# Gated attention with a mixture of experts: the lists of tokens added up by matrix products, routing in two batches, and a new order of the attention's steps

## Chip, cores and metric

One core of one Trainium2 chip runs the whole program. The metric is the time of one execution in microseconds of the device (us), as the median of several runs. Lower is better.

## What is computed

A recurrent attention (4 batches, 8 heads, 768 steps, head size 48) writes 3072 rows of 384 numbers, and each row then goes through the one of 8 experts that its gate picks:

```python
for t in range(S):
    S_re, S_im = ar*S_re - ai*S_im + outer(k[t], v[t]), ar*S_im + ai*S_re
    y[t] = q[t] @ S_re                 # rows x of the second half
e_idx = argmax(x @ w_gate, 1)
for e in range(8):
    m = e_idx == e
    out[m] = gate_w[m] * eom[m, e] * (relu(x[m] @ w1[e]) @ w2[e])   # 384 -> 1024 -> 384
```

gate_w is the softmax weight of the chosen expert and eom a sigmoid gate. The inputs are float32; products of the experts are made of a high and a low part of each factor.

## The kernel before

The rows are cut into 24 chunks of 128 (chunk 0 to 23, six to a batch). For each chunk the attention takes some fifty steps, each a Python function of one to 48 instructions: loads (la, lb), the logarithms of the decay (Ln, Ex, D1, Sq, L1, D2, E2, D3), running sums on TensorE (cd, cp), sines and cosines, the products of k and q with them (kc, qc), their transposes (trk, trq) and the copies of these out of PSUM (ck, cq), scores (sc), the mask (mk), the state (st, sd, cps), the output (va), its copy (xt), the product that gives rows and gate logits (ro), and then the copy of the rows (xn), their store to DRAM (xs) and the sum of the logits (gt). A table written out by hand (ORDER) lists the steps; every engine takes its instructions in this order. A letter v or a behind a step moves a copy to VectorE, or a rounding or an absolute value to ScalarE.

Routing stands in the same table. Chunks 0 to 19 are routed in BATCHES of 6, 6, 6 and 2. For each batch, R1 to R4 (choose and weigh) find on VectorE each row's expert, its rank among that expert's rows, and its gate weight; two matrix products (R2) count the rows before it. GpSimd then works out the row's address in a table in DRAM (pl: places), and writes one pair (row id, gate weight) per row with an indirect DMA, one per chunk (el: enter_list). K1 to KV rank the experts by size. Before the first expert starts, rr reads its list back (read_ranked), si makes ids of it, and ga fetches the rows with four indirect DMAs. Chunks 20 to 23 (the TAIL) are added in another way: P1, PK, P2 make 0/1 rows, fl adds their rows to the first expert's input by matrix products, and lists/add put their entries in the other lists after the first expert has begun. After the attention, TensorE runs the experts one after another (experts: up_products, down_products), and the other lists are read from DRAM.

Six PSUM banks are handed round between the steps in the order of the table, so a step that holds a bank for long keeps the next from starting. Two constants used below: NS = 4 slots to a list row, NP = 116 list rows.

Of the kernel before, what the change touches and what calls it, by code (L numbers as in the profile page):

```python
# [1535 lines left out]
```

## Time and profile before

| | us |
|---|---|
| median of 3 runs | 484.17 |
| lowest and highest run | 483.86, 489.08 |
| the profiled execution | 489.85 |
| its span, first to last instruction | 488.1 |

The profiled execution is 1.75 us longer than its span, and 5.68 us longer than the median. Busy shares of the span: PE (TensorE matrix products) 95%, PEld (its weight loads) 86%, DVE (VectorE) 70%, ACT (ScalarE) 62%, POOL (GpSimd) 25%. A busy PE is a modelled figure, since matrix products overlap; the share of PEld tells better how full TensorE is. The granted clock was at the higher of its two levels (2.4 GHz) throughout, but for the last slice. The attention fills the time up to about 246 us, the experts the rest.

### The profile page before, as it was taken

The page shows a single profiled execution, that of the slowest core. Times are in us where ns is not written, and L with a number is a line of the kernel's source. Part 1 is how long each engine was busy: PE and PEld are TensorE (multiplying, and loading weights), DVE is VectorE, ACT ScalarE, POOL GpSimd, SP SyncE. Part 2 cuts the span into 40 slices and gives each one's busy share as a digit, 9 for nine tenths or more (in the row PEclk, how much of TensorE's full clock was granted, in tenths as well). Part 3 has the DMA queues.
Part 4 walks back from the last instruction along what each step waited for, and adds up shares of the span by engine and source line. Part 5 has one row for each costly group of instructions (what it writes and reads, how often), then busy time and mean ns, then how long its engine had stood idle before and what let it go on. Part 6 is the DMA issues. An engine that isn't in the chain of part 4 may idle for free.

```text
span 488.1 us, 11400 instructions
## 1 busy us (share of the span) xinstructions
PE 466.0 (95%) x4350; PEld 418.9 (86%) x4350; DVE 340.6 (70%) x693; ACT 304.4 (62%) x569; POOL 123.0 (25%) x161
## 2 busy tenths in 40 slices
PE   8998999899999979999999999999999999999991
PEld 4786777778888768888888999999999999999991
DVE  4499999999999979998799764362735536283210
ACT  7759889989998768743266565362735536283330
POOL 5100000013300540183401645324251222021112
PEclk9999999999999999999999999999999999999997
DMA  8974354524543231003835789283552817220001
GB/s 277 319 234 133 97 153 127 178 81 108 95 162 99 67 67 36 34 19 132 266 111 185 187 240 296 69 252 110 151 181 59 279 49 243 69 92 26 25 25 49
DMA packets 47757, 65.66 MB, mean 135 GB/s; under 512 B 11711, under 2 KB 39498, under 8 KB 47668
## 3 DMA queue, kind: packets, MB, share of 16 engines
q1 hardware_dynamic: 39540, 55.01, 36.9%
q0 software_dynamic: 8128, 9.42, 6.9%
q8 instruction: 62, 1.02, 0.9%
q14 instruction: 27, 0.22, 0.1%
HBM read 53.92 MB, written 9.88 MB: 131 GB/s over the span
## 4 chain that ended last, share of the span: by engine, by line
PE 57%; DVE 17%; issue 16%; POOL 4%; ACT 2%; DMA 1%; POOLq 0%; another core or an unknown queue 0%; SPq 0%; DVEq 0%; ACTq 0%
PE b L1208 8%; PE b L186 7%; PE b L1193 6%; PE xo L1193 6%; PE b L668 5%; PE st L1208 4%; POOL out_dram L1227 3%; DVE scores L673 3%; PE xo L700 3%; PE b L338 2%; PE b L613 2%; PE xo L706 2%; PE st L683 2%; PE st L861 2%; DVE kc L645 2%
## 5 line engine op out<-in xcount | busy, mean ns | idle before, releaser
L1227 POOL DMA_INDIRECT out_dram<-y,sid x28 | 33.3, 1190 | 116.9 <-ACT y L1249 113.4
L668 PE MATMUL b<-qt,kt 96*128 96x128 f32 x384 | 48.3, 279 | 1.7 <-ACT qt L657 1.3
L668 PEld LDWEIGHTS b<-qt,kt 96*128 96x128 f32 x384 | 44.9, 192 | 5.3 <-ACT qt L657 2.0
L1097 POOL DMA_INDIRECT rows<-xd,sid x28 | 35.1, 1255 | 51.4 <-DVE gate L1080 24.9
L1290 DVE SCALAR_TENSOR_TENSOR hl<-xo,hh 128x464 fp32r<-128x464 f32 (+7 forms) x32 | 18.9, 589 | 38.4 <-ACT hh L1289 29.2
L1290 DVE SCALAR_TENSOR_TENSOR hl<-b,hh 128x464 fp32r<-128x464 f32 (+7 forms) x32 | 18.9, 590 | 37.9 <-ACT hh L1289 33.3
L1289 ACT ACTIVATE hh<-b 128x464 fp32r<-128x464 f32 (+7 forms) x32 | 16.5, 517 | 37.5 <-PE b L1193 34.9
L1208 PE MATMUL b<-hh,w2h 128*128 128x392 f32 (+6 forms) x112 | 38.5, 344 | 0.0
L1208 PE MATMUL b<-hh,w2l 128*128 128x392 f32 (+6 forms) x112 | 38.4, 343 | 0.0
L1289 ACT ACTIVATE hh<-xo 128x464 fp32r<-128x464 f32 (+7 forms) x32 | 16.6, 520 | 33.4 <-PE xo L1193 26.3
L700 PE MATMUL xo<-scores,v 128*48 128x128 f32 x384 | 36.2, 277 | 1.0 <-DVE scores L673 1.0
L585 POOL COPY rcs<-rcs 24x48 f32<-24x48 f32 (+2 forms) x10 | 3.7, 373 | 126.3 <-DMA rcs<-re 81.6
L1193 PE MATMUL b<-xh,w1h 128*128 128x392 f32 (+6 forms) x93 | 33.6, 361 | 0.0
L1193 PE MATMUL xo<-xh,w1h 128*128 128x392 f32 (+6 forms) x93 | 32.9, 353 | 0.0
L673 DVE TENSOR_TENSOR scores<-b,mask 128x512 f32<-128x512 f32 x48 | 31.7, 680 | 1.4 <-PE b L668 0.7
L1193 PE MATMUL b<-xl,w1h 128*128 128x392 f32 (+6 forms) x93 | 31.6, 340 | 0.0
L1193 PE MATMUL xo<-xl,w1h 128*128 128x392 f32 (+6 forms) x93 | 31.6, 340 | 0.0
L1193 PE MATMUL xo<-xh,w1l 128*128 128x392 f32 (+6 forms) x93 | 31.6, 339 | 0.0
L1193 PE MATMUL b<-xh,w1l 128*128 128x392 f32 (+6 forms) x93 | 31.5, 339 | 0.0
L706 PE MATMUL xo<-qt,state 96*48 96x128 f32 x320 | 31.2, 272 | 0.2 <-DVE state L688 0.2
L318 DVE TENSOR_TENSOR w2l<-raw,w2h 128x512 fp32r<-128x512 f32 x42 | 26.6, 686 | 4.3 <-ACT w2h L317 4.3
L318 DVE TENSOR_TENSOR w1l<-raw,w1h 128x512 fp32r<-128x512 f32 x42 | 26.6, 686 | 4.2 <-ACT w1h L317 4.2
(281 smaller groups left out, 1320.3 us busy)
## 6 DMA issues: line engine op xcount, KB each, us to landing
raw<-in_moe_w_dram SPq DMA_DIRECT2D x32, 768.0 KB
ar<-in_a_re_dram SPq DMA_DIRECT2D x24, 192.0 KB
ai<-in_a_im_dram SPq DMA_DIRECT2D x24, 192.0 KB
q<-in_q_dram SPq DMA_DIRECT2D x24, 192.0 KB
k<-in_k_dram SPq DMA_DIRECT2D x24, 192.0 KB
v<-in_v_dram SPq DMA_DIRECT2D x24, 192.0 KB
xd<-xn SPq DMA_DIRECT2D x24, 192.0 KB
rows<-rows SPq DMA_DIRECT2D x1, 768.0 KB
```

The costliest lines, as they stand in the source:

```text
L186: return nc.tensor.transpose(out=out, in_=in_, identity=ident[p0:p0 + n, p0:p0 + n])
L318: nc.vector.tensor_tensor(out=lo[:, s], in0=raw[:, s], in1=hi[:, s].bitcast(F32), op=ALU.subtract)
L668: nc.tensor.matmul(sp[:, j * P:(j + 1) * P], cats_t["k"][i % 2][:D2, h, :], cats_t["q"][i % 2][:D2, h, :], start=True, stop=True)
L673: nc.vector.tensor_tensor(out=scores[i % 2][:, 4 * hh:4 * hh + 4, :], in0=of(("sc", i, hh)).rearrange("p (h t) -> p h t", t=P), in1=mask.u ...
L700: nc.tensor.matmul(op[u * DP:u * DP + D, j * P:(j + 1) * P], vt[:, h * D:(h + 1) * D], scores[i % 2][:, h, :], start=True, stop=(cc == 0))
L706: nc.tensor.matmul(op[u * DP:u * DP + D, j * P:(j + 1) * P], xs[:D2, h * D:(h + 1) * D], cats_t["q"][i % 2][:D2, h, :], start=False, stop= ...
L1097: ins = nc.gpsimd.indirect_dma_start(out=rows[e % 2][:n, i, :], out_offset=None, in_=xd[:known], in_offset=bass.IndirectOffsetOnAxis(ap=id ...
L1193: nc.tensor.matmul(used(up[:, :sizes[e]], n), w[:, kt, :], used(x[:, kt, :], n), start=(m == 0), stop=(m == 3 * KT - 1))
L1208: nc.tensor.matmul(used(accs[kt][:, :sizes[e]], n), w[:, cs], used(a, n), start=(ft == 0 and s == 0), stop=(ft == FT - 1 and s == 2))
L1227: ins = nc.gpsimd.indirect_dma_start(out=out, out_offset=bass.IndirectOffsetOnAxis(ap=id_of(e, i, n, loaded), axis=0), in_=y[:n, :], in_of ...
L1289: nc.scalar.activation(out=hh, in_=up[:, :cap], func=AF.Relu)
L1290: nc.vector.scalar_tensor_tensor(out=hl, in0=up[:, :cap], scalar=0.0, in1=hh.bitcast(F32), op0=ALU.max, op1=ALU.subtract)
```

## The change

The lists no longer go through DRAM. Each row has a list row `row` and a column `col` (expert and slot). GpSimd makes a 0/1 matrix of columns and multiplies it with three values (row id, high and low part of the gate weight); ScalarE makes a 0/1 matrix of list rows as relu(1 - |iota - row|) (step ir); TensorE adds up the product of the two over the chunks of a batch in one bank (Lp), and VectorE takes it over (Ld). Batches are now 18 and 2 chunks. si picks the first expert's list out of it, and in_places the others'; the last expert's list alone still takes a way through DRAM. ORDER is a new table; which copies go to which engine has changed in it as well: on VectorE 5 ck fewer, 7 cq more, 6 xn fewer, 2 cps more, 1 xt fewer, and 1 rounding and 4 absolute values more, with the opposite on ScalarE.

```diff
-BATCHES = ((0, 6), (6, 6), (12, 6), (18, 2))
+BATCHES = ((0, 18), (18, 2))
...
+set.0 la.0.0.0 la.1.0.0 la.0.0.1 la.2.0.0 la.1.0.1 la.2.1.1 Ln.0.0 la.2.1.0 Ln.1.0 la.2.0.1 Ex.0.0 lb.0.0 Ex.1.0 lg
...
+        if halves:
+            c = slice(c0, c0 + n)
+            nc.vector.tensor_copy(out=gate_hi[:, c], in_=entry[:, c, 1])
+            nc.vector.tensor_tensor(out=gate_lo[:, c], in0=entry[:, c, 1], in1=gate_hi[:, c].bitcast(F32), op=ALU.subtract)
...
             def pl(b):
-                places(sml, *BATCHES[b], eng=nc.gpsimd)
+
+                c0, n = BATCHES[b]
...
+                eng.tensor_tensor(
+                    out=at_, in0=iota[:, :E * NS].unsqueeze(1).broadcast_to([P, n, E * NS]),
+                    in1=col.unsqueeze(2).broadcast_to([P, n, E * NS]), op=ALU.subtract)
+                eng.tensor_scalar(out=at_, in0=at_.bitcast(F32), scalar1=0.0, scalar2=None, op0=ALU.is_equal)
...
+            def ir(b):
...
+                for i in range(n):
+                    function(out=is_row[:, i, :], in_=iota[:, :NP], func=AF.Abs, bias=row[:, i:i + 1])
+                function(out=is_row, in_=far, func=AF.Relu, scale=-1.0, bias=b_one)
...
             def el(b):
-                enter_list(*BATCHES[b])
...
+                for x, val in enumerate((entry[:, c, 0], gate_hi[:, c].bitcast(F32), gate_lo[:, c])):
+                    nc.gpsimd.tensor_tensor(
+                        out=cols[:, :, x, :], in0=is_col, in1=val.unsqueeze(2).broadcast_to([P, n, E * NS]), op=ALU.mult)
+
+            def Lp(b):
...
+                for c in range(n):
+                    nc.tensor.matmul(
+                        sp[:NP, :3 * E * NS], is_row[:, c, :], cols[:, c].rearrange("p x y -> p (x y)"),
+                        start=(c == 0), stop=(c == n - 1))
...
-            def rr():
-                read_ranked(0, 1)
-
             def si():
+                part = sml.tile([P, NS, E], F32, name="part")
+                nc.vector.tensor_tensor(
+                    out=part[:NP], in0=listed_by[:NP, 0].rearrange("p e i -> p i e"),
+                    in1=is_at[:NP, 0, :].unsqueeze(1).broadcast_to([NP, NS, E]), op=ALU.mult)
+                nc.vector.tensor_reduce(out=slots[:NP, 0, :, 0], in_=part[:NP], axis=AX.X, op=ALU.add)
                 slot_ids(0, 1)
...
-                for k in range(KT):
-                    turned(out=new_whole[:, k, :], in_=by_slot[:, k * P:(k + 1) * P])
...
-            for ins in read_ranked(1, E):
-                behind(ins, tail["gathered"])
...
+            def in_places(pool):
+
+                nc.vector.tensor_tensor(out=listed_by[:NP, 1], in0=listed_by[:NP, 1], in1=listed_by[:NP, 2], op=ALU.add)
+                part = pool.tile([P, E, NS, E], F32, name="part")
+                shape = [NP, E, NS, E]
+                for x in range(2):
+                    nc.vector.tensor_tensor(
+                        out=part[:NP], in0=listed_by[:NP, x].rearrange("p e i -> p i e").unsqueeze(1).broadcast_to(shape),
+                        in1=is_at[:NP].unsqueeze(2).broadcast_to(shape), op=ALU.mult)
+                    nc.vector.tensor_reduce(out=slots[:NP, :, :, x], in_=part[:NP], axis=AX.X, op=ALU.add)
```

GpSimd, before, from the routing of the third batch to the fetch of the first expert's rows:

```order
L1038 TENSOR_TENSOR row<-row,shift 128x6
L1039 TENSOR_SCALAR addr<-row 128x6
L1043 DMA table<-entry,addr 3712x2 x6
L793 MEMSET rows_2847 128x384
L1032 TENSOR_SCALAR row<-rank 128x2
...
L1043 DMA table<-entry,addr 3712x2 x2
L1097 DMA rows_2847<-xd,sid 116x384 x4
```

GpSimd, after, the same place: no table is written, and wide element-wise work stands there (cols is the matrix of columns, 18 chunks of 32).

```order
L781 TENSOR_TENSOR col<-col,off 128x18
L785 TENSOR_TENSOR cols_2628<-iota,col 128x18x32
L788 TENSOR_SCALAR cols_2628<-cols_2628 128x18x32
L808 TENSOR_TENSOR cols_2628<-cols_2628,entry 128x18x32
L808 TENSOR_TENSOR cols_2628<-cols_2628,gate_hi 128x18x32
L808 TENSOR_TENSOR cols_2628<-cols_2628,gate_lo 128x18x32
...
L1152 DMA rows_2951<-xd,sid 116x384 x4
```

The 20 table writes are gone, and five operations over 576 elements and five over 64 have come.

TensorE, after, around the adding up of the first 18 chunks (row 816; L687 is the state of chunk 21, L338 the rows of chunk 20, L672 scores):

```order
L183 MATMUL b_219<-ident,kc_198 96x128 x4
L687 MATMUL st<-v,kc_199 32x48 x24
...
L374 MATMUL b_215<-run,ones_b 128x16
L338 MATMUL b_217<-comb,xt_210 128x112 x4
L816 MATMUL b_219<-cols_2628,is_row_2715 116x96 x18
L672 MATMUL b_218<-qt_205,kt_203 128x128 x4
```

Whatever TensorE has to do for chunks 21 to 23 now stands behind these 18 products, which need GpSimd's cols and ScalarE's is_row.

TensorE, before, at the end of the attention (L668 scores, the last ones; L338 the rows of chunks 20, 21, 22, 23; L700 and L706 the output; L910 the transposes of the first expert's fetched rows):

```order
L668 MATMUL b_213<-qt_200,kt_198 128x128 x4
L338 MATMUL b_211<-comb,xt_206 128x112 x4
L338 MATMUL b_212<-comb,xt_207 128x112 x4
L700 MATMUL xo<-scores_204,v 48x128 x2
...
L338 MATMUL b_210<-comb,xt_206 128x112 x4
...
L338 MATMUL b_213<-comb,xt_207 128x112 x4
L910 MATMUL b_211<-ident,rows_2847 128x64 x8
```

TensorE, after, the same place:

```order
L338 MATMUL b_218<-comb,xt_211 128x112 x4
L672 MATMUL b_217<-qt_205,kt_203 128x128 x4
L672 MATMUL b_214<-qt_205,kt_203 128x128 x4
L704 MATMUL xo<-scores_208,v 48x128 x2
...
L338 MATMUL b_219<-comb,xt_210 128x112 x4
...
L338 MATMUL b_217<-comb,xt_211 128x112 x4
L967 MATMUL b_214<-ident,rows_2951 128x64 x4
```

The rows of chunks 20 and 21 now come ahead of the last scores, so that two of four such products are left between those and the transposes.

## Rows read from the trace of the kernel before

**Rows 1.** Busy time of each engine by stretch (stretch, its length, then the engines).

```profile
12.00:40.00 28.00, 27.80 (x365) 22.07 (x363) 20.98 (x37) 19.47 (x36) 1.90 (x5) 1.00 0.79 258
40.00:200.00 160.00, 152.72 (x1887) 125.61 (x1886) 152.12 (x288) 140.42 (x246) 24.23 (x34) 1.00 0.38 105
200.00:234.00 34.00, 32.67 (x491) 29.16 (x490) 31.83 (x83) 15.90 (x32) 16.42 (x24) 1.00 0.20 63
234.00:246.00 12.00, 10.64 (x161) 9.36 (x160) 8.71 (x35) 4.15 (x9) 5.31 (x4) 1.00 0.81 275
246.00:440.00 194.00, 193.70 (x1164) 189.86 (x1164) 112.26 (x225) 104.02 (x211) 61.37 (x50) 1.00 0.54 161
```

**Rows 2.** VectorE's waits over the span: for whom, us in total, times, longest.

```profile
DVE ai L624 <- ACT rnd L331: 4.6, 4, 3.3
```

**Rows 3.** VectorE in the four stretches that route the third batch of 6 chunks.

```profile
199.36:200.97 1.61, 1.40 (x9) 1.00 0.66 245
...
sum 2.91, DVE 2.57; mean DVE 0.64
```

**Rows 4.** VectorE's copies by form: count, busy us, mean ns.

```profile
L657 DVE COPY kt<-b 96x512 f32<-96x512 f32 x21 | 14.1, 678 | 0.0
L657 DVE COPY xn<-b 128x384 f32<-128x384 f32 x15 | 8.2, 544 | 0.0
L631 DVE TENSOR_SCALAR rnd<-ai 128x384 int32<-128x384 int32 x12 | 4.2, 346 | 0.0
```

**Rows 5.** GpSimd's groups: the table writes, and the wide operations that it has.

```profile
L1043 POOL DMA_INDIRECT table<-entry,addr x20 | 24.8, 1239 | 18.3 <-DVE scores L673 11.9 <-issue 4.9 <-DVE st L657 1.3
L231 POOL TENSOR_SCALAR_AFFINE_SELECT comb<-comb 128x192 f32<-128x192 f32 x2 | 1.2, 616 | 0.0
L215 POOL IOTA iota<- 128x464 f32 x1 | 0.5, 517 | 0.0
L199 POOL CAST tri_r<-tri_l 128x128 fp32r<-128x128 f32 x1 | 0.3, 279 | 0.0
```

**Rows 6.** All engines in order of time (start, us): two operations that meet.

```profile
199.58 0.21 DVE L354 TENSOR_TENSOR dl<-logits,mx 128x48 f32<-128x48 f32 x1
...
199.81 0.21 POOL L585 COPY rcs<-rcs 24x48 f32<-24x48 f32 x1 [21.70 <-PE b L186]
199.82 0.27 DVE L356 SCALAR_TENSOR_TENSOR ge<-dl,desc 128x48 f32<-128x48 f32 x1
```

**Rows 7.** GpSimd in order of time: first and last address operation of the third batch.

```profile
205.73 0.84 POOL L1032 TENSOR_SCALAR row<-rank 128x6 f32<-128x6 f32 x1 [5.70 <-DVE rank L378]
...
209.46 1.46 POOL L1039 TENSOR_SCALAR addr<-row 128x6 uint32<-128x6 f32 x1
```

**Rows 8.** ScalarE's groups by form.

```profile
L537 ACT ACTIVATE sq<-ai 128x384 f32<-128x384 f32 x5 | 2.6, 523 | 0.6 <-DVE ai L533 0.4
...
L331 ACT ACTIVATE ex<-dl 128x48 f32<-128x48 f32 x3 | 0.7, 241 | 0.0
```

**Rows 9.** TensorE in order of time, end of the attention and start of the experts.

```profile
234.92 1.94 PE L338 MATMUL b<-comb,xt 128*128 128x112 f32 x16
...
245.86 1.58 PE L910 MATMUL b<-ident,rows 64*128 64x64 f32 x20
...
248.60 0.28 PE L926 MATMUL b<-row,k 128*128 128x208 f32 x1
248.71 0.28 PE L926 MATMUL b<-row,q 128*128 128x208 f32 x1
...
276.84 0.92 PE L186 MATMUL b<-ident,rows 110*128 110x110 f32 x8
```

**Rows 10.** GpSimd in order of time: the first expert's fetches (first, last), the second's first.

```profile
235.31 1.37 POOL L1097 DMA_INDIRECT rows<-xd,sid  x1 [8.06 <-DVE sid L1076]
...
240.22 1.31 POOL L1097 DMA_INDIRECT rows<-xd,sid  x1 [0.30 <-issue]
266.41 1.07 POOL L1097 DMA_INDIRECT rows<-xd,sid  x1 [24.88 <-DVE gate L1080]
```

More of the change, by code (lines that the diff above doesn't have):

```diff
@@ L387, in at_once, with weigh @@
                 return end.value
[L389 removed]
+    def weigh(pool, c0, n, dl, oh, tag="", halves=False):
         def small(name, shape):
@@ L762, in pl @@
             def pl(b):
-                places(sml, *BATCHES[b], eng=nc.gpsimd)
-            def el(b):
-                enter_list(*BATCHES[b])
+                c0, n = BATCHES[b]
+                c = slice(c0, c0 + n)
+                pool = early if b < len(BATCHES) - 1 else sml
+                row, col, off = [pool.tile([P, n], F32, name=name) for name in ("row", "col", "off")]
+                eng = nc.gpsimd
+                eng.tensor_scalar(
+                    out=row, in0=rank[:, c], scalar1=-1.0 / NS, scalar2=0.5 - 0.5 / NS, op0=ALU.mult, op1=ALU.add)
@@ new lines, in pl @@
+                eng.tensor_scalar(out=row, in0=row, scalar1=ROUND, scalar2=-ROUND, op0=ALU.add, op1=ALU.add)
+                eng.tensor_scalar(out=off, in0=row, scalar1=float(NS), scalar2=float(E * NS), op0=ALU.mult, op1=ALU.add)
+                eng.tensor_scalar(out=col, in0=first[:, c], scalar1=float(-NS), scalar2=None, op0=ALU.mult)
+                eng.tensor_tensor(out=col, in0=col, in1=rank[:, c], op=ALU.add)
+                eng.tensor_tensor(out=col, in0=col, in1=off, op=ALU.add)
+                pool = early if b < len(BATCHES) - 1 else sml
@@ new lines, in pl @@
+                cols = pool.tile([P, n, 3, E * NS], F32R, name=f"cols{n}")
+                at_ = cols[:, :, 2, :]
+                eng.tensor_tensor(
+                    out=at_, in0=iota[:, :E * NS].unsqueeze(1).broadcast_to([P, n, E * NS]),
+                    in1=col.unsqueeze(2).broadcast_to([P, n, E * NS]), op=ALU.subtract)
+                eng.tensor_scalar(out=at_, in0=at_.bitcast(F32), scalar1=0.0, scalar2=None, op0=ALU.is_equal)
+                tail["list", b] = row, cols
+            def ir(b):
+                n = BATCHES[b][1]
+                row, _ = tail["list", b]
+                is_row = (early if b < len(BATCHES) - 1 else sml).tile([P, n, NP], F32R, name=f"is_row{n}")
+                far = is_row.bitcast(F32)
+                for i in range(n):
+                    function(out=is_row[:, i, :], in_=iota[:, :NP], func=AF.Abs, bias=row[:, i:i + 1])
+                function(out=is_row, in_=far, func=AF.Relu, scale=-1.0, bias=b_one)
+                tail["rows", b] = is_row
@@ L1012, in lists @@
                     pass
+                in_places(pool)
                 yield
@@ L1015, in lists @@
                 slot_ids()
+                ready["second rows"] = gather(1, CAPS[1])
+                slot_gates()
+                nc.sync.dma_start(
+                    out=by_rank.rearrange("(p s) y -> p s y", s=NS), in_=slots[:KT * P // NS, E - 1])
+                nc.sync.dma_start(out=whole, in_=by_rank.rearrange("(k p) y -> p k y", p=P))
+                yield
                 nc.vector.tensor_scalar(
                     out=whole_sid, in0=whole[:, :, 0], scalar1=float(NONE), scalar2=None, op0=ALU.add)
-                ready["second rows"] = gather(1, CAPS[1])
-                slot_gates()
                 yield
@@ L1308, in experts @@
                     if loaded and e == 0:
-                        for _ in range((0, 2, 1, 0, 0, 0, 0, 0)[ft]):
+                        for _ in range((0, 2, 1, 0, 0, 0, 1, 0)[ft]):
                             next(last)
```

199 lines of the change are left out of this document (98 added, 101 removed).

## The prediction

> **What bounds the kernel now.** I read the busy times by stretch first [rows 1], to see which engine has no time left where. From 246 to 440 us, in the experts, TensorE's weight loads are busy for 189.86 of 194 us: TensorE is full, and its work there is hardly touched. So the change can act only through the moment at which the experts start, and the reader is to look at the attention. There, from 40 to 200 us, VectorE is busy for 152.12 of 160, while weight loads fill 125.61 and ScalarE 140.42; from 200 to 234 VectorE has 31.83 of 34 and ScalarE only 15.90. VectorE bounds the attention, and a microsecond of its work is worth nearly one of the total. It stands still for 7.0 us between 12 and 40, 7.9 between 40 and 200, 2.2 between 200 and 234 and 3.3 between 234 and 246, 20.4 in all; a new order can win back only from these. Next I read its waits [rows 2]: the longest single one, 3.3 us at the start, is for a rounding on ScalarE. Last, the order of time at the end of the attention [rows 9, 10]: what stands between the last scores (234.9) and the transposes of the first expert's rows (245.86), a chain of small steps with VectorE a quarter idle.
>
> **The change part by part.** *Routing on VectorE.* One batch of 6 takes 15 small operations, which hold VectorE for 2.91 us, as four stretches show [rows 3]; three such batches take 8.7. One batch of 18 replaces them, again 15 operations, of which 11 read or write 144 elements a row for 48. The slope is that of the copies: (678 - 544) ns over 128 elements, 1.05 ns each [rows 4], so 0.10 us more for each of the 11: 2.9 + 1.1 = 4.0. New are four operations for the halves of the gate weights and four that take the lists over (Ld twice, si twice), small ones at the 0.2 that an operation of that stretch takes: 1.6. Together 5.6 for 8.7: -3.1 us. Bounds: -3.8 if the new ones hide in dependent waits, -2.0 if each takes 0.35.
>
> *Copies that change engines.* An operation holds VectorE for about 0.1 us less than its duration, since the next starts before it ends. Widths of 512: -5 ck, +7 cq, -1 xt, +1 at 0.58; of 384: -6 xn, +2 cps, +1 rounding, -3 at 0.44; +4 absolute values at 0.25 [rows 4]. 0.58 - 1.32 + 1.0 = +0.3 us. ScalarE gets the opposite, which its 18 idle us between 200 and 234 hide.
>
> *GpSimd's work, and what it does to VectorE.* Twenty table writes of 1.24 us go [rows 5]; nobody but the first list's read waited for them, so that alone is worth nothing. Ten element-wise operations come, five of them over 576 elements. The trace has none like these. From below, iota: 517 ns for 464 elements, 1.1 ns each, 0.64 us for 576; from above, the select: 616 ns for 192, 3.2 ns each, 1.85 us. I take the cast, 279 ns for 128, 2.2 ns each, 1.26 us, which like the new operations reads SBUF, without the select's pattern. Four of the five have two inputs. Where GpSimd and VectorE meet, the trace shows both slowed: a 48-wide step of VectorE took 0.27 beside a GpSimd copy, its neighbour of the same width 0.21 [rows 6]; GpSimd's address operations over 6 elements ran from 0.84 to 1.46 beside VectorE's products [rows 7]. With operations of 0.2 us this cost VectorE nothing; with 1.26 us it can. In the stretch of pl.0 and el.0, VectorE has five products of 768 with both inputs in SBUF (kc, qc) and some small ones. Nothing is lost if none of them meets a wide operation, and five times 1.26, 6.3 us, if each of the five wide ones holds VectorE for all its length. I take a quarter, +1.5, nearer to the row of 0.06 lost than to a full block.
>
> The Trainium skill has a rule that speaks against the change here: by "SBUF — State Buffer", section "Who interferes with whom", a VectorE instruction with two SBUF inputs and a GpSimd instruction that reads SBUF exclude each other for the whole of the one that started first. The trace agrees as far as its 0.06 us goes, and no run shows a wide operation. By that rule each of the five would hold VectorE for half its length on average, 3.2 us, and the whole sum below would be -0.9 in place of -2.6, 483.3 us.
>
> *ScalarE's matrix of list rows (ir.0).* 18 operations over 116 elements and one over 2088. With (523 - 241) ns over 336 elements, 0.84 ns each [rows 8], a short one lasts 0.30, and 0.2 where they overlap; the long one takes 1.95. In all 5.6 to 7.4 us, during which the copies ck.21.1, xt.20 and ck.22.1 queue behind it on ScalarE. The order leaves it about 6.5 (VectorE's work in that place, next paragraph, less what precedes ir.0). I take +0.3, between 0 and +1.5.
>
> *TensorE's 20 products (Lp).* 208-wide products of the same kind follow each other by 0.11 us [rows 9]: 2.2 us. They lie in a stretch in which weight loads leave 4.8 of 34 us free: 0, or +2.2 if that cover is gone. What matters is their wait. Behind the 18 on TensorE stand the scores and transposes of chunks 21 to 23, and for these all of VectorE's rest. They need GpSimd's five wide operations. From the rank of the 18 chunks to that place VectorE has five products of 768 (0.85 each), a 384-wide product, two sd, two cps and an xn (0.44), three copies and two masks (0.58) and some 15 small operations (0.2): 12.4 us. GpSimd needs six small operations, which go by the 5.2 us of the seven before [rows 7], 4.4, and five at 1.26 with 0.1 between: 11.2. So TensorE does not wait, with 1.2 us to spare.
>
> *End of the attention.* Two of the four products that make rows (16 instructions, 1.94 us [rows 9]) move from behind the last scores to before them, where TensorE has room. VectorE's share of this (the sums and low parts of chunks 20 and 21, about 1 us) moves as well, and there VectorE has none. 1.94 - 1.0: -1.0 us, between -2.5 and +0.5. What could be late next are the fetched rows: ids, then four fetches that last 6.2 us from 235.31 to 241.53 [rows 10]. Before, transposes followed 10.5 us after the first fetch; the shorter end leaves some 9.5, still more than fetches and landing need by TensorE's start. The list no longer goes through 8 table writes, a read of the table and the register with the expert's number; that takes waits off a path that had none on TensorE.
>
> *Start.* k is loaded ahead of q and the first rounding goes to VectorE itself; of the 3.3 us wait [rows 2] I count -0.3, between -2 and +0.5.
>
> *Experts.* Three transposes go, at 0.11: -0.3. in_places adds about 1.4 us to VectorE before the fetch for the second expert, now at 266.41 [rows 10]; its transposes stand at 276.84 [rows 9], and VectorE is busy for 112 of 194: nothing, or +1 if that fetch lands last.
>
> The sum: -3.1 + 0.3 + 1.5 + 0.3 - 1.0 - 0.3 - 0.3 = -2.6 us. It is made on the profiled execution, 489.85, giving 487.25. The median is 484.17; no row tells where the other 5.68 us went, so I carry the difference over: 481.6 us.
>
> **Rivals.** *GpSimd is late, and the attention waits at the 18 products.* If the wide operations cost the select's 1.85 us, with 0.1 between, they last 9.8; with 4.4 for the small ones 14.2; and if five of them first wait for a product of VectorE (0.95), 18.9. It decides from the 12.4 us at which TensorE arrives: then VectorE has nothing left that needs no scores, and 6.5 us are lost in place of the +1.5: -2.6 - 1.5 + 6.5 = +2.4, 486.6. For it speak the 1.46 us for 6 elements [rows 7]; against it, that GpSimd wins as many of these meetings as it loses, and that at the cast's price it is done in time.
>
> *The new order closes VectorE's gaps.* The 20.4 idle us [rows 1] come from waits like that of 3.3. If a fourth of them goes, 5.1 us, in place of the -1.3 taken for start and end, the sum is -6.4: 477.8. For it speaks that ScalarE has less to do late and that two batches fewer hand products between TensorE and VectorE; against it, that between 40 and 200 only 7.9 us are idle.
>
> *Nothing comes of it.* If VectorE's saved work only turns into longer waits for TensorE and ScalarE (busy for 140 of 160), 484.2.
>
> **How the numbers follow.** The forecast has 0.5, its own range -4.5 to +0.5 (479.7 to 484.7); closed gaps 0.24; nothing 0.13; GpSimd late 0.13. About 1%, 4.8 us, is what a measurement of this kernel tells from no change. Faster by more: all of the closed gaps but a fifth (0.19), and 0.08 of the forecast's tail: 0.27. Slower by more: the GpSimd case needs 7.4 us where it gives 2.4, some 0.06 of its 0.13, with 0.02 for an order that waits elsewhere: 0.08. Same: 0.65. The range takes in the closed gaps to -7.4 and the late GpSimd to +2.4: 476.8 to 486.6.
>
> **What would show it.** Right: VectorE's busy time before the experts about 3 us lower and its share still above 90% up to the last scores; the 18 products starting without a wait on GpSimd; the wide operations at 0.9 to 1.6 us; transposes of the first expert's rows 2 to 3 us earlier. Wrong: an idle VectorE of several us around 215 to 225 that ends with the 18 products; products kc and qc longer than 0.95 there; transposes that wait for a fetch; an expert stretch longer than before.

## The result, and the profile after

| | before, us | after, us |
|---|---|---|
| median of 20 runs each | 485.41 | 491.22 |
| lowest and highest | 482.75, 489.08 | 487.54, 496.22 |
| the profiled execution | 489.85 | 493.61 |
| first transposes of the experts' rows | 245.86 | 246.57 |

The ratio of after to before is 1.0107, 95% interval 1.0076 to 1.0138: about 1% slower, where 481.6 us and "within 1%" had been forecast. One thing is needed to understand it: the executions of the kernel before fall into two groups, 482.8 to 484.2 and 485.3 to 489.1 us here (an earlier and a later time below), sets of runs differ in which is the commoner, and the profile that the prediction read, 489.85, goes with the later; those of the kernel after spread without such a gap.

Busy time by stretch of the kernel after, columns as in [rows 1]:

```profile
12.00:40.00 28.00, 28.00 (x359) 22.44 (x357) 20.90 (x36) 20.63 (x40) 1.81 (x4) 1.00 0.85 288
40.00:200.00 160.00, 153.27 (x1874) 128.61 (x1873) 150.54 (x259) 139.57 (x241) 10.82 (x8) 0.98 0.34 104
200.00:234.00 34.00, 32.20 (x503) 28.96 (x502) 32.27 (x88) 20.94 (x50) 15.81 (x23) 1.00 0.17 61
234.00:246.00 12.00, 10.82 (x167) 9.97 (x167) 9.70 (x39) 6.64 (x15) 5.43 (x4) 1.00 0.88 286
246.00:440.00 194.00, 191.16 (x1135) 186.73 (x1135) 110.83 (x222) 98.78 (x201) 59.72 (x48) 0.99 0.54 159
```

Between 40 and 200 VectorE (third number with a count) is idle for 9.5 us, against 7.9 in [rows 1]; in the experts weight loads lost 3.1 us (186.73 for 189.86). VectorE's busy time up to the first transposes, overlaps counted once, is 218.98 us after and 218.84 before, where about 3 us less had been forecast.

VectorE's waits in the kernel after (for whom, us in total, times, longest), beside [rows 2]:

```profile
DVE ai L537 <- DMA ai<-in_a_im_dram: 4.0, 2, 3.0
DVE ai L628 <- ACT rnd L331: 2.9, 4, 1.3
DVE rnd L625 <- PE b L617: 2.7, 1, 2.7
DVE ai L612 <- DMA carry<-ai: 2.1, 3, 1.3
DVE state L692 <- PE st L687: 2.0, 1, 2.0
DVE logits L342 <- ACT xn L661: 2.0, 5, 0.6
```

The rounding wait is shorter (2.9 for 4.6), and five more stand beside it. The first, for a load, stands where the kernel before waited 4.0 us for ScalarE, at the same step. A wait for the carry, a row of 1.5 KB that travels by a DMA of SyncE's queue, does not stand in the trace of before.

GpSimd of the kernel after in order of time (start, us), from the rank of the 18 chunks to the end of the matrix of columns, the place of [rows 7] and the new work beside [rows 5]:

```profile
210.78 0.84 POOL L775 TENSOR_SCALAR row<-rank 128x18 f32<-128x18 f32 x1 [12.24 <-DVE rank L378]
...
214.15 1.19 POOL L785 TENSOR_TENSOR cols<-iota,col 128x576 fp32r<-128x576 f32 x1
215.43 1.66 POOL L788 TENSOR_SCALAR cols<-cols 128x576 fp32r<-128x576 f32 x1
217.18 3.22 POOL L808 TENSOR_TENSOR cols<-cols,entry 128x576 fp32r<-128x576 f32 x1
220.35 2.55 POOL L808 TENSOR_TENSOR cols<-cols,gate_hi 128x576 fp32r<-128x576 f32 x1
222.99 1.19 POOL L808 TENSOR_TENSOR cols<-cols,gate_lo 128x576 fp32r<-128x576 f32 x1
```

The five wide operations have the same size and last from 1.19 to 3.22 us; all is done at 224.18, 13.4 us after the rank. TensorE comes to the 18 products at 226.24 and does not wait for them (TensorE in order of time, with the transposes of [rows 9]):

```profile
226.24 2.01 PE L816 MATMUL b<-cols,is_row 128*116 128x96 f32 x18
228.09 2.01 PE L672 MATMUL b<-qt,kt 96*128 96x128 f32 x16
...
246.57 1.51 PE L967 MATMUL b<-ident,rows 64*128 64x64 f32 x20
```

VectorE beside these operations, in order of time:

```profile
222.47 0.48 DVE L354 TENSOR_TENSOR dl<-logits,mx 128x16 f32<-128x16 f32 x1
222.98 0.17 DVE L356 SCALAR_TENSOR_TENSOR ge<-dl,desc 128x16 f32<-128x16 f32 x1
223.19 0.17 DVE L358 TENSOR_REDUCE first<-ge 128x2 f32<-128x16 f32 x1
223.39 0.82 DVE L360 TENSOR_TENSOR oh<-desc,first 128x16 bf16<-128x16 f32 x1
```

Two small operations with two inputs were stretched, from 0.17 to 0.48 and 0.82; its products of 768 kept their 0.94 to 0.95. Each of the two ended within 0.05 us of the GpSimd operation that had begun before it (222.95 for 222.90, 224.21 for 224.18).

### The profile page after: what moved, and what is told of

The parts are those of the page before. It is cut to its first block, busy times and chain, and to the rows that moved or that the text cites. A ratio compares the mean times of both kernels' runs of the same rounds, so it can differ in the third digit from the quotient of the medians.

```text
span 491.8 us, 11341 instructions
## 1 busy us (share of the span) xinstructions
PE 468.1 (95%) x4365; PEld 425.0 (86%) x4365; DVE 341.9 (70%) x675; ACT 310.2 (63%) x585; POOL 109.0 (22%) x135
## 4 chain that ended last, share of the span: by engine, by line
PE 53%; DVE 15%; issue 14%; DMA 6%; POOL 5%; ACT 5%; POOLq 0%; SPq 0%; DVEq 0%; ACTq 0%
PE b L183 8%; PE b L1263 7%; PE b L672 6%; PE xo L1248 6%; PE b L1248 5%; PE st L1263 4%; POOL out_dram L1282 3%; PE b L338 3%; PE b L617 3%; PE xo L704 2%; DMA raw<-in_moe_w_dram 2%; DMA rows<-xd,sid 2%; PE b L566 2%; PE st L687 2%; PE xo L710 2%
## 5 line engine op out<-in xcount | busy, mean ns | idle before, releaser
L672 PEld LDWEIGHTS b<-qt,kt 96*128 96x128 f32 x384 | 47.1, 197 | 5.7 <-DVE qt L661 1.7
L672 PE MATMUL b<-qt,kt 96*128 96x128 f32 x384 | 50.0, 284 | 0.5 <-DVE qt L661 0.5
L589 POOL COPY rcs<-rcs 24x48 f32<-24x48 f32 (+2 forms) x10 | 11.3, 1131 | 172.9 <-DMA rcs<-re 135.0
L318 DVE TENSOR_TENSOR w2l<-raw,w2h 128x512 fp32r<-128x512 f32 x42 | 26.6, 685 | 7.6 <-ACT w2h L317 7.6
L317 ACT CAST w2h<-raw 128x512 fp32r<-128x512 f32 x42 | 23.3, 623 | 10.7 <-DMA raw<-in_moe_w_dram 10.7
```

The lines of the kernel that those rows point to most:

```text
L318: nc.vector.tensor_tensor(out=lo[:, s], in0=raw[:, s], in1=hi[:, s].bitcast(F32), op=ALU.subtract)
L672: nc.tensor.matmul(sp[:, j * P:(j + 1) * P], cats_t["k"][i % 2][:D2, h, :], cats_t["q"][i % 2][:D2, h, :], start=True, stop=True)
```

## Experiments

In each set the kernel before ran beside the others on the same chip, and ratios are to it (they are not the ratios of the two medians). What a trace tells about the attention is put as the start of the experts' first transposes ("transposes"), 245.86 in [rows 9].

### Lists and order apart

The old order with the new lists (batches 18 and 2), and the new order with the old ones (batches 6, 6, 6, 2):

```diff
 # old order, new lists
-BATCHES = ((0, 6), (6, 6), (12, 6), (18, 2))
+BATCHES = ((0, 18), (18, 2))
-R1.0 ... R3.0 ... el.0 ... R1.1 ... el.1 ... R1.2 ... pl.2 ... el.2 ... rr
+R1.0 ... pl.0 ... el.0 ... ck.20.1 ir.0 ro.19 ... Lp.0 trk.22.1 xt.20 Ld.0
```

> Lists added up on TensorE and two batches, but every other step in the order and on the engines of before. Theory 1 (the new order loses the time, by gaps early in the attention that also halve TensorE's clock): no slower than before, ratio 0.992 to 1.000. Theory 2 (the new lists lose it, in the attention by GpSimd's wide operations, in the experts by the later fetch for the second expert): ratio 1.006 to 1.014.

> The new order and its copies on the engines that it names, but lists by table writes to DRAM in four batches as before. Theory 1 (order): ratio 1.008 to 1.018, with the half clock at 48 to 56 us. Theory 2 (lists): ratio 0.995 to 1.004 and an expert stretch as long as in before.

> The changed kernel, once more. Ratio 1.008 to 1.014. If the half clock at 48 to 56 us and the 2.1 us standstill of TensorE at 301 us belong to the change, this second profile shows both again; if they are accidents of one execution, it shows neither, and the time must be lost elsewhere.

Before 489.48. Old order with new lists 496.26, ratio 1.0157 (1.0113 to 1.0202), transposes 250.42. New order with old lists 516.56, 1.0556 (1.0521 to 1.0591), transposes 270.21. After again 490.55, 1.0022 (0.9994 to 1.0051), transposes 247.32; before again 490.17, transposes 246.44. Neither half is a gain by itself, in the places that the other's steps were given here. In this set, where before ran at its later time, the change made no difference that can be told from none. What stood in the way in the old order is in TensorE's waits of that run:

```profile
PE b L189 <- ACT qt L667: 5.1, 1, 5.1
```

and in ScalarE's order of time there:

```profile
212.41 5.20 ACT L337 ACTIVATE is_row<-iota,row 128x116 fp32r<-128x116 f32 x18
217.65 2.04 ACT L337 ACTIVATE is_row<-is_row,b_one 128x2088 fp32r<-128x2088 f32 x1
219.59 0.56 ACT L667 COPY qt<-b 96x512 f32<-96x512 f32 x1
```

The matrix of list rows held ScalarE for 7.2 us, and a copy that TensorE wanted stood behind it.

### The clock, and the second expert's row ids

In three of the four profiles of the kernel after, TensorE's granted clock was at 1.2 GHz for part of the 8 us from 48 on (0.57, 0.58 and 0.79 of 2.4 GHz on average). Two edits: idle products (wm, nine more groups of eight) between the steps of 40 to 48 us, and in the experts the row ids ahead of the gate weights.

```diff
 # fillers
-ri.2 gt.1 trq.2.0 ... cq.2.1 cd.5 ... kc.2 Ln.4.0 cd.4
+ri.2 gt.1 wm.20 trq.2.0 ... cq.2.1 wm.21 wm.22 wm.23 cd.5 ... kc.2 Ln.4.0 wm.24 cd.4
 # row ids first
-                in_places(pool)
+                steps = in_places(pool)
+                next(steps)
                 yield
-                yield from add(pool, bank)
+                new = yield from add(pool, bank)
+                new(0)
                 slot_ids()
                 ready["second rows"] = gather(1, CAPS[1])
+                next(steps)
+                new(1)
+                new(2)
                 slot_gates()
```

> The changed kernel with nine more groups of idle products (eight of 128x128 each, 0.45 us a group) on TensorE between 39 and 48 us, where it waits for VectorE for 3.6 us; nothing else differs. Theory 1 (the gap lets the clock fall, and the half clock from 48 to 56 us costs the attention its gain): granted clock 1.00 there, the attention ends 3 to 4 us earlier (transposes at 242.5 to 244), total 3 to 4 us below e2_after. Rival (VectorE's gaps cost it, the clock is beside the point, since VectorE has work of its own meanwhile): the clock stays up, but the end of the attention moves by under 1 us.

> The changed kernel, but with the gates' half of in_places and of the additions behind the second expert's row ids, so that its fetch starts about 1.3 us earlier (267.5 in place of 268.9). Theory (that later fetch, through the third expert's rows, delays a piece of weights to 301.6 and TensorE stands for 2 us): standstill at 301 us under 0.8 us, expert stretch 1.3 to 2.5 us shorter. Rival (the weights are late for a reason of their own): standstill as long as in e2_after.

> Both edits together. If both theories hold: 5 to 6 us below e2_after, and below before. If only the first: 3 to 4; if neither: as e2_after.

Before 490.91. After 490.98, 0.9996 (0.9963 to 1.0028); fillers 490.6, 0.9989 (0.9958 to 1.002); row ids first 490.11, 0.998 (0.9948 to 1.0012); both 489.45, 0.995 (0.9921 to 0.9978; one of its twelve executions took 930.36 us and is left out of the ratio). Transposes: after 246.49, fillers 245.00, row ids first 243.98, both 244.10. The clock is not the main cause: in this set's profile of the kernel after it stayed up, and the transposes still came at 246.49; with the fillers it stayed up too, they came 1.5 us earlier, and the whole was no shorter. The same stretch in the trace of the result, and in this set's trace of after:

```profile
40.00:48.00 8.00, 4.87 (x27) 2.76 (x25) 8.00 (x16) 7.44 (x18) 0.40 (x1) 1.00 0.35 110
48.00:56.00 8.00, 7.55 (x78) 6.80 (x80) 5.97 (x12) 6.29 (x14) 0.21 (x1) 0.57 0.34 103
```

```profile
40.00:48.00 8.00, 5.08 (x29) 2.96 (x27) 8.00 (x16) 7.42 (x17) 0.33 (x1) 1.00 0.32 99
48.00:56.00 8.00, 6.89 (x138) 5.93 (x141) 8.00 (x17) 7.41 (x16) 2.41 (x1) 1.00 0.38 117
```

VectorE lost 2.0 us in the one (5.97 of 8) and nothing in the other, where it waited elsewhere: 3.7 us for the carry instead of 2.1. The row ids first changed nothing in the attention, and yet its transposes came 2.5 us earlier: profiles of one and the same order of the attention differ by that much (243.98 here, 245.79 to 247.32 in the four of after). Counted from the transposes, the second expert's fetch moved from 22.6 us in this set's after to 21.2, and TensorE no longer stood still at 302; it stood 0.77 us at 276 instead, for a fetched row. Only the two together gave something, 0.5%, and only against the later of before's times.

### The carry behind the loads, and the lump on ScalarE

Here before ran at its earlier time, 484.44 in 29 runs. In the trace of after, SyncE issues the carry behind three loads:

```profile
91.54 1.27 SPq L522 DMA_DIRECT2D ar<-in_a_re_dram  x3
92.91 0.57 SPq L608 DMA_DIRECT2D carry<-ai  x1
```

and VectorE takes it at 97.08, after a wait (VectorE in order of time):

```profile
97.08 0.55 DVE L612 SCALAR_TENSOR_TENSOR ai<-carry,ai 1x384 f32<-1x384 f32 x1 [1.33 <-DMA carry<-ai]
```

The edit moves the loads of two groups behind the carry; a second kernel has the fillers and the row ids as well; a third is the old order with new lists, ScalarE's matrix in six parts.

```diff
 # loads late
-ri.9 la.9.0.0 trk.7.1 ... Ex.6.0 la.9.1.0 ... fr.9 la.9.2.0 ... ck.7.1 cdma.9 D1.6.0
+ri.9 trk.7.1 ... Ex.6.0 ... fr.9 ... ck.7.1 cdma.9 la.9.0.0 la.9.1.0 la.9.2.0 D1.6.0
 # six parts
-                for i in range(n):
-                    function(out=is_row[:, i, :], ...)
-                function(out=is_row, in_=far, func=AF.Relu, ...)
+                for i0 in range(0, n, 3):
+                    for i in range(i0, i0 + m):
+                        function(out=is_row[:, i, :], ...)
+                    function(out=is_row[:, i0:i0 + m], in_=far[:, i0:i0 + m], func=AF.Relu, ...)
+                    yield
```

> The changed kernel with five loads of decay factors (la.8.0.0, la.8.1.0, la.9.0.0 to la.9.2.0, 192 KB each, needed much later) moved on SP from ahead of the transfers of a carry (cdma.7, cdma.9) to behind them; nothing else. Theory 1 (the new order sends the carry's 1.5 KB behind big loads, and VectorE waits for it, 2.1 to 3.7 us in three profiles): VectorE's wait for the carry below 1 us in all, transposes of the first expert's rows 1.5 to 2.5 us earlier (at 244 to 245), ratio to before 0.3 to 0.5 per cent lower than the changed kernel's on these chips (0.995 to 0.999). Rival (the clock): the carry's wait goes, but the end of the attention stays at 246.5, wherever a half clock is seen before 60 us.

> Fillers, the row ids first, and the loads behind the carries. If the losses are separate: transposes at 243.5 to 244.5 in every execution, few half clocks, ratio 0.990 to 0.995. If the loads' place is all that matters in the attention: as e3_loads_late within 0.5 us at the transposes.

> Lists on TensorE and two batches in the order of before, as e1_oldorder_newlists (which ended the attention at 250.4 us, after TensorE had waited 5.1 us for a copy that stood on ScalarE behind the 19 operations of ir.0), but with ir.0 cut into six parts that stand between ScalarE's copies. If ir.0's length on ScalarE was all that was lost there: attention ends 5 us earlier (transposes at 245 to 246), ratio 0.996 to 1.003. If the lists cost more than that in the old order: transposes at 248 or later, ratio above 1.008.

Loads late 488.28, 1.0088 (1.0049 to 1.0127), transposes 243.69; the wait that was left:

```profile
DVE ai L618 <- DMA carry<-ai: 0.9, 2, 0.6
```

The waits for the carry are shorter, 0.9 us in all for 2.1 to 3.7 in the four profiles of after, and the carry of the rows shown was taken 3.2 us after its issue for 4.2. That this is what brought the transposes forward, 2.8 us ahead of the 246.49 that the kernel after had in the set before this one, is not shown: the row ids first had them at 243.98 with the loads in their old place, and the kernel after did not run in this set. All three edits 489.16, 1.0105 (1.007 to 1.014), transposes 243.72: nothing on top. Six parts 499.33, 1.0274 (1.0216 to 1.0333), transposes 250.93: that the lump of 7.2 us alone was at fault in the old order fell; the parts, between 210 and 224, still made TensorE wait 2.92, 1.35 and 0.70 us.

The most telling of this set is before itself, 483.66, with a profile of 483.91 and transposes at 239.21. At one and the same step, VectorE in the profile that the prediction read:

```profile
169.97 0.54 DVE L608 SCALAR_TENSOR_TENSOR ai<-carry,ai 1x384 f32<-1x384 f32 x1
172.99 0.55 DVE L688 TENSOR_TENSOR state<-st,rc 96x384 f32<-96x384 f32 x1 [2.49 <-PE b L668]
```

and in this one:

```profile
168.29 0.54 DVE L608 SCALAR_TENSOR_TENSOR ai<-carry,ai 1x384 f32<-1x384 f32 x1
168.79 0.55 DVE L688 TENSOR_TENSOR state<-st,rc 96x384 f32<-96x384 f32 x1
```

What GpSimd does beside the wait of 2.49 us, in the first:

```profile
168.47 1.32 POOL L1043 DMA_INDIRECT table<-entry,addr  x1 [1.29 <-DVE st L657]
170.10 1.25 POOL L1043 DMA_INDIRECT table<-entry,addr  x1 [0.31 <-issue]
171.66 0.98 POOL L1043 DMA_INDIRECT table<-entry,addr  x1 [0.30 <-issue]
172.94 0.97 POOL L1043 DMA_INDIRECT table<-entry,addr  x1 [0.30 <-issue]
```

The state's other inputs were there: TensorE's products for st ended at 170.41, and ScalarE copied no rc between 168.5 and 173; what the row names as releaser (scores) the step does not read. Three gaps over 1 us and two smaller ones, beside table writes and the MEMSET that follows the last of a batch, add up to 5.6 us in the profile read (489.85 - 484.17 had been 5.68; the transposes of the two profiles lie 6.65 apart). At one of them, 1.12 us before 221.50, VectorE waited for a product of TensorE, and TensorE itself had stood still twice, for nothing that the profile shows:

```profile
220.06 0.29 PE L683 MATMUL st<-v,kc 128*32 128x48 f32 x5 [0.34 <-issue]
220.83 0.40 PE L683 MATMUL st<-v,kc 128*32 128x48 f32 x11 [0.48 <-issue]
```

None of these gaps is in the execution of 483.91 us, and there the writes were the longer:

```profile
L1043 POOL DMA_INDIRECT table<-entry,addr x20 | 30.0, 1500 | 18.0 <-DVE scores L673 11.6 <-issue 4.3 <-DVE st L657 1.3
```

30.0 us for the 24.8 of [rows 5]: GpSimd loses 5.2 us in the one execution, and VectorE 5.6 in the other. GpSimd has time to spare, VectorE has none. The second profile of before at its later time (before again, above) lies between: writes of 27.6 us, and gaps of 1.03, 1.75 and 1.11 at the same three steps.

### The table writes taken out, and doubled

```diff
 # no writes
-el.0 ... el.1 ... el.2
+...
 # writes twice
                 enter_list(*BATCHES[b])
+                if b < 2:
+                    enter_list(*BATCHES[b], group="twice", to=table2)
```

The first leaves out the writes of 18 chunks into the table, so the lists of these rows are not made; the second writes the first two batches also into a table that nobody reads.

> The kernel before without the 18 table writes of GpSimd's first three batches (the lists stay empty but for the last batch, so few rows are fetched and the experts' figures mean nothing here; only the attention is compared). Theory (where the kernel before is at 490 us, its VectorE is held at three or four places, 5.6 us in all, and each of these lies beside a table write): attention ends at 239 to 240 us whatever the kernel before shows beside it, without a gap of VectorE of over 0.8 us between 100 and 225 us. Rival (the two times of the kernel before come from something else): where before is at 490, it ends at 245 to 246 with the same gaps.

> The kernel before with the 12 table writes of its first two batches issued twice (the second time into a table that nobody reads). Theory: more writes beside VectorE's steps, so it is held more often: at least one further gap of 1 us or more between 117 and 190 us, total 1 to 4 us above before. Rival: total as before within 1 us, since nobody waits for the writes themselves.

Before 491.23, after 490.65 (0.9989, 0.9963 to 1.0016). No writes 482.64, 0.9831 (0.9808 to 0.9854), transposes 241.65 (239 to 240 had been expected), none of the gaps. Of the 8.6 us to before, 4.2 to 4.8 lie in the attention, against the transposes at 245.86 and 246.44 of the two profiles of before with gaps; where the rest lies is not shown, since few rows are fetched without lists, and no profile of before was taken in this set. Writes twice took 495.73 us in one execution and 503.37 to 506.33 in the other five, where 1 to 4 us above before had been expected; no ratio is given. In the profile, of 504.02, the transposes came at 259.85, and the clock was down in part (134 to 137 and 184 to 195). Its VectorE:

```profile
126.40 0.35 DVE L634 TENSOR_SCALAR rnd<-ai 128x384 int32<-128x384 int32 x1
132.09 0.55 DVE L691 TENSOR_TENSOR state<-st,rc 96x384 f32<-96x384 f32 x1 [5.34 <-remote]
```

and its GpSimd:

```profile
127.64 0.97 POOL L1048 DMA_INDIRECT table<-entry,addr  x1 [0.30 <-issue]
128.91 0.97 POOL L1048 DMA_INDIRECT table<-entry,addr  x1 [0.30 <-issue]
130.19 0.97 POOL L1048 DMA_INDIRECT table<-entry,addr  x1 [0.30 <-issue]
131.47 0.97 POOL L1048 DMA_INDIRECT table<-entry,addr  x1 [0.30 <-issue]
```

The gap of 1.08 us at this place in the profile read before became 5.34, while the writes go on at 0.97 us each. TensorE did not get on either: beside the doubled writes of the second batch, between 184 and 192.5, it stood still six times, for 0.76 to 1.01 us, for nothing that the profile shows. The first two:

```profile
185.13 0.29 PE L703 MATMUL xo<-scores,v 128*48 128x128 f32 x1 [0.82 <-issue]
186.54 0.45 PE L709 MATMUL xo<-qt,state 96*48 96x128 f32 x2 [1.01 <-issue]
```

So it is shown that the gaps come and go with the table writes and grow with their number, though no instruction on the path waits for their data: 18 of them cost the attention 4.2 to 4.8 us against executions with the gaps (the early execution of before, with all of them, ended it at 239.21). By what they hold the other engines up, no view tells.

### Lists on TensorE in better places

If the writes cost that much and the new lists need none, a version in the order of before should beat both. The first has six parts of the matrix spread from chunk 19 on and the products later, the second the lists in before's four batches.

```diff
 # old order, better places
+xn.18v ir.0.0 ir.0.1 rnd.23a ... trk.20.1 ir.0.2 ... ck.20.1 ir.0.3 ... sc.20.0 ir.0.4 ... ck.21.0 ir.0.5 ... ck.22.1v Lp.0 ... ck.23.1 Ld.0
 # four batches
+BATCHES = ((0, 6), (6, 6), (12, 6), (18, 2))
```

> Lists on TensorE in the order of the kernel before, batches of 18 and 2, ScalarE's matrix of list rows in six parts spread from chunk 19 to chunk 21, the 18 products placed behind the copy of chunk 22's keys and their take-over later still. The same kernel without its table writes (writes left out) had its transposes at 241.65. Theory 1 (the lists on TensorE cost the attention about what the writes cost, wherever they stand, since VectorE has no free time to take them over): transposes at 246 to 251, total 490 to 499. Theory 2 (only the places were bad, so that ScalarE and TensorE stood still): transposes at 240 to 243, total 482 to 486, faster than both kernels in a session where before takes 489 to 491, ratio 0.985 to 0.995.

> Lists on TensorE in the order of the kernel before with its own four batches of 6, 6, 6 and 2: GpSimd's wide operations are 192 elements instead of 576, ScalarE's matrix of list rows stands in pieces of about 2.4 us, and each batch has its own products and take-over; VectorE's routing is not shortened (three batches of 15 small operations, 8.7 us, for 4.0). Theory 1 (lists cost what the writes cost): transposes at 246 or later, total 490 and more. Theory 2 (bad places, or one lump of 7.2 us on ScalarE): transposes at 240 to 244, total 482 to 487. Between this run and the other one: if this is the faster by 2 us or more, the batch of 18 is what hurt.

Before 490.9. Better places 491.82, 1.0012 (0.9985 to 1.0038), transposes 247.94; four batches 499.53, 1.0148 (1.0104 to 1.0192), transposes 250.55. The lists cost the attention at least what the writes cost. Where, the output product of each chunk tells: with better places chunk 16 begins at 184.6 us and chunk 18 at 201.5, as in the run without writes (185.8 and 201.1); chunk 20 then at 224.7 for 220.9, chunk 22 at 238.4 for 232.6. The time saved up to 200 us is given back in the 45 us after it, where VectorE stands still (better places, then without writes):

```profile
200.00:234.00 34.00, 29.73 (x461) 26.00 (x462) 29.64 (x73) 22.68 (x55) 15.78 (x23) 1.00 0.17 56
```

```profile
200.00:234.00 34.00, 33.17 (x515) 29.93 (x514) 31.20 (x77) 15.45 (x33) 11.98 (x19) 1.00 0.30 104
```

ScalarE has 7.2 us more there (22.68 for 15.45), and TensorE waits 1.5 and 0.7 us for copies of k that ScalarE makes late. With four batches TensorE once waits for GpSimd's columns as well, 1.6 us. No version that makes the lists beats the kernel before at its earlier time.

## Why the prediction was wrong, point by point

**The failing step is the last one, "no row tells where the other 5.68 us went, so I carry the difference over".** Rows did tell: the gaps beside table writes, 5.6 us, were in the very profile. With it fell the term put at nothing for the edit that takes the writes away, "nobody but the first list's read waited for them, so that alone is worth nothing": without 18 of the writes the transposes came at 241.65, for 245.86 and 246.44 where the gaps stand, and an execution of before without the gaps takes 484. The 5.68 us go with the writes, which the change removes, so they could not be taken off the time after once more. Without that step the text's own 487.25 stands against 491.22; the rest of the miss is in the sum. The question that was missing is why two executions of the same program differ by 5 us, and the view that answers it is VectorE's idle time by gap, each with what GpSimd does beside it.

**Then the sum itself, -2.6 us, came out as +3.8** between the two profiled executions (493.61 - 489.85): +0.7 up to the transposes, +4.4 in the experts, -1.3 after the last product begins. And up to the transposes the 5.6 us of the gaps had gone too, so about 6 us came back there. In three other sets, with before at its later time, the two kernels took the same (0.9989 to 1.0022). By its terms:

- Routing, -3.1 forecast: its operations on VectorE up to the ids, the tail's apart, add up to 11.5 us before (61) and 9.5 after (39), -2.0, the weak end of the bounds of -3.8 to -2.0 (and with all new ones hidden the text's own figures give -4.7, not -3.8). The batch of 18 held it for 4.4 us where 4.0 was taken, and the batch of 2 met GpSimd's wide work: 1.0 of the 9.5 is the stretch that stands below under its own term. Without it the term is right.
- Copies, +0.3: by tile, the durations up to the transposes changed by +4.7 (qt), -3.8 (xn), -3.4 (kt), +1.9 (rnd), +1.1 (st) and -0.7 (xt), -0.3 in all, and one copy of rows, 0.5, now stands behind the transposes. Right.
- VectorE held by GpSimd's wide work, +1.5: the stretched small operations cost about 1.0 (0.48 + 0.82 for twice 0.17). The size is near, the price list was not: 1.19 to 3.22 us per operation for 1.26. By the rule of the Trainium skill ("SBUF — State Buffer", "Who interferes with whom"), a VectorE instruction with two SBUF inputs and a GpSimd instruction that reads SBUF exclude each other. The trace agrees: the two stretched operations ended with the GpSimd operation that had begun before them, and GpSimd's 3.22 and 2.55 us stand beside products of VectorE that kept their 0.94. It was mostly GpSimd that paid.
- ir.0, 5.6 to 7.4 us on ScalarE: 7.2. Lp: no wait, 2.1 us after GpSimd was done. The rival of a late GpSimd did not happen, but by luck in part: GpSimd took 13.4 us for the 11.2 taken, and TensorE came 15.5 us after the rank for 12.4 (the operations listed for that figure add up to 12.8).
- End of the attention, -1.0: from the last scores' end to the transposes it was 10.8 us before (235.08 to 245.86) and is 8.4 after (238.2 to 246.57); but chunk 22's output product moved from 236.8 to 238.1, so the shorter end only paid for a later beginning.
- Start, -0.3: nothing was won. VectorE is busy for 25.94 of the first 40 us, 26.32 before; the waits there have other names, 4.0 us for the first load where 4.0 for ScalarE stood, 2.7 for a running sum where 3.3 for the rounding stood.
- The rival of closed gaps had the sign wrong. VectorE's idle time up to the transposes was 26.0 us in the profile read, 19.6 in the early execution of before, 26.6 after. The old gaps went, and the new order has others: 2.1 to 3.7 us for the carry, 2.0 where the clock was down, 3.3 for logits behind ScalarE.
- Experts, -0.3 forecast, +4.4 measured (236.2 us from the transposes to the last product for 231.82), of which 1.5 in a profile of after without any drop of the clock there (233.34). The two other profiles of before have 232.7 and, with the clock down in part, 235.4, so only some of this is the change. in_places took 2.16 us for 1.4, the ids came at 267.81 and the fetch at 268.86 for 266.41; the third expert's fetches, from 288.25 for 285.73, then ran beside the weight piece issued at 289.93, which was cast only at 301.56. That ScalarE wait of 5.18 (at most 3.9 in the three profiles of before) left TensorE idle, and the clock fell after it (0.66 on average from 305 to 310):

```profile
303.75 0.60 PE L183 MATMUL b<-ident,yt 128*116 128x128 f32 x3 [1.94 <-ACT y L1304]
```

The other profiles of after show 1.50, 0.57 and 1.29 there, those of before nothing or 0.60. That fetch and piece collide is argued from their times and not shown; with the ids first the standstill went, and another of 0.77 came at 276, and with the fillers beside them one of 0.79 stood at 301.

Of what "would show it", the busy share held (32.27 of 34) and the 18 products did not wait, but busy time did not fall, three of the wide operations lay above 1.6 us, the transposes came 0.7 us later, and the experts grew, the last of the signs that the text had named for being wrong.

What stays open: what decides whether the writes hold the other engines up or are themselves the longer (sets run one after the other on one chip showed both), by what the one holds the other, and why one and the same order of the attention ends between 243.98 and 247.32.

## What to carry to other kernels

When the profiled execution is several us away from the median, find the gaps that make the difference before a sum is made on it: the change may be about to remove them. Work on GpSimd that nobody waits for was not free here while it ran beside the engine that bounds the stage, and taking it away paid nothing, since its replacement stands in the last, densest part of that stage. Before a gain of 2 us is put down to an edit, look how far profiles of one and the same order lie apart. A small transfer that the bounding engine waits for is worth moving ahead of bulk loads in its queue: the wait shrank, though the gain in time could not be told apart.

## What the runs showed of the hardware

- An indirect DMA that writes 128 pairs holds GpSimd for 0.97 to 2.13 us in the profile read, and for up to 3.54 in the early execution. While several follow each other, VectorE can stand still for 2.5 us (six writes) to 5.3 us (twelve) before a product that reads one operand from PSUM and one from SBUF, and TensorE for 0.34 to 1.01 us at a time between its products. By the same section of the Trainium skill's "SBUF — State Buffer", a VectorE instruction with at most one SBUF input, outside its 2-port modes, does not contend with GpSimd. Here such an instruction stood still, and the measurement decides; but whether it was SBUF that held it is not shown, since TensorE stood still as well.
- The same GpSimd product over 576 elements took 1.19 us and 3.22 us, a few us apart, beside VectorE's work.
- A row of 1.5 KB issued at 92.91 behind three loads was taken at 97.08, after a wait; with the loads behind it, it was issued at 90.96 and taken at 94.16, and the waits for all carries fell from 2.1 to 0.9 us.
- The granted clock fell to 1.2 GHz after stretches of 8 us (40 to 48) in which weight loads were busy for 2.76, 2.85 and 3.04 us, and stayed at 2.4 GHz after one with 2.96: from these figures alone it can't be told when it falls.
